# Moving VectorE work of the first batches of a linear-attention and mixer kernel to GpSimd and ScalarE

## The chip, the cores and the metric

One Trainium2 chip, one core. The time is device microseconds of one execution of the whole program; less is better. The engines are TensorE (PE in the profile), VectorE (DVE), ScalarE (ACT), GpSimd (POOL) and SyncE (SP, here only a queue of DMA issues).

## The reference

Three stages on 8 batches of 576 tokens and 512 channels (8 heads of 64), all float32:

```
q_s = softmax(q, over head_dim);  k_s = softmax(k, over tokens)
kv  = einsum('bhsd,bhse->bhde', k_s, v);  x = einsum('bhsd,bhde->bhse', q_s, kv)
xk  = mu_k*x + (1-mu_k)*x_prev;  xr = mu_r*x + (1-mu_r)*x_prev     # x_prev: one token earlier
x1  = sigmoid(xr @ w_r) * (maximum(xk @ w_k, 0)**2 @ w_v)
u   = x1 + real(fft(fft(x1, axis=1), axis=2))
out = u + maximum(layernorm(u) @ w_ch1, 0) @ w_ch2
```

The weights of the second and third stage come as float64.

## The kernel before, in words

Every large product is done as three matmuls on float32r parts: a value is rounded to its high part, the low part is value less high part, and high x high, low x high and high x low are summed in PSUM. A float64 weight is loaded as raw integers, turned into float32 by two ScalarE (L69, L73) and two VectorE instructions (L74, L77), and split by a ScalarE cast (L83) and a GpSimd subtraction (L84). Five raw buffers go round, so the next weight load, issued by SP, waits for an L84.

The first part of the program, on which the change acts, is attention and the first mixing, batch by batch:

- Keys, per batch and head pair (`hp` 0 to 3): `k_load`, `k_max` (VectorE maximum over the tokens within a partition), `k_col` (TensorE transpose, VectorE maximum `kc` for each channel, then `kd`, the identity with its rows scaled by `kc`), `k_sub` (a matmul of `ones` with `kd` spreads the maxima over all partitions; VectorE subtracts them from the keys), `k_exp` (ScalarE), `k_kv` (TensorE), `k_out` (VectorE reciprocal `rs`, then `kvh` on ScalarE and `kvl` on VectorE).
- Queries, per batch and group of tokens (`L`, `T`, `B`): `q_load`, `q_max` (VectorE), `q_sub` (subtracts the maximum), `q_exp` (ScalarE), `q_sum` (VectorE), `q_mul` (GpSimd), `q_tr` (TensorE transposes, high part on ScalarE, low part on VectorE), `q_x` (product with `kvh`, `kvl`; ScalarE copies it into `xb`, one buffer for each parity of batch).
- Mixing, per chunk `c` of 384 tokens (three chunks in two batches) and head pair: `mix_diff` forms the difference of a token and its neighbour (`dt`), `mix_part` forms `xm = dt*(1-mu) + x` once for `xk` and once for `xr` and splits each (`hi` on ScalarE, `lo` on GpSimd). Then `m_wk` (L440 to L442, eight column blocks), `m_r` (L456 to L458) and `m_wv` (L471 to L473).

Batch 0 and chunk 0 stand first in the program text, with the weight pieces behind them; batch 1 and all later work is placed by slots (`sched`, `aux`) between the matmuls of the chunk before. The text's order is not the last word: the program is built with

```
    with tile.TileContext(nc, schedule_with_timeline_sim=True) as tc:
```

so that the order of each engine's queue is planned at build from a model of the costs. Each queue then runs in order.

After this part come the two transforms (as matmuls with tables) and the last product, which fill the second half of the time with TensorE work.

The functions that the diff touches, with their line numbers:

Of the kernel before, what the change touches and what calls it, by code (L numbers as in the profile page):

```python
# [14 lines left out]
AF = mybir.ActivationFunctionType  # L15
ALU = mybir.AluOpType
# [26 lines left out]
def kernel(ctx, tc, q, k, v, mu_k, mu_r, w_k, w_v, w_r, w_ch1, w_ch2, tab_s, tab_d, out):  # L43
    nc = tc.nc
# [7 lines left out]
    ident = const.tile([P, P], F32, name="ident")  # L52
# [35 lines left out]
    with ExitStack() as ph:  # L88
# [20 lines left out]
        def spare(i, dtype, name):  # L109
            return wp.tile([P, 2 * D], dtype, tag=f"wv{i}", name=name, bufs=1)  # L110
# [5 lines left out]
        xb = [p1.tile([P, NHP, XW], F32, name=f"xb{i}") for i in range(2)]  # L116
# [5 lines left out]
        omu = p1.tile([P, 2, NHP], F32, name="omu")  # L122
# [64 lines left out]
        def k_col(n, hp):  # L187
            km = state.pop(("km", n, hp))
            pm = ps.tile([P, 512], F32, tag="pa", name=f"pm{n}_{hp}", bufs=4)
            nc.tensor.transpose(pm[:, 0:P], km, ident)  # L190
            kc = p1.tile([P, 1], F32, tag="kc", name=f"kc{n}_{hp}", bufs=2)
            nc.vector.tensor_reduce(out=kc, in_=pm[:, 0:P], axis=AX.X, op=ALU.max)
            kd = p1.tile([P, P], F32, tag="kd", name=f"kd{n}_{hp}", bufs=2)
            nc.vector.tensor_scalar(kd, ident, kc, None, op0=ALU.mult)
            state["kd", n, hp] = (kd, pm)

        def k_sub(n, hp):
# [71 lines left out]
        def q_sub(n, g):  # L269
            qt = state["q", n, g]  # L270
            np_, nj = qt.shape[0], qt.shape[2]
            qm = state.pop(("qm", n, g))
            (nc.vector if n < 2 else nc.gpsimd).tensor_tensor(
                out=qt,
                in0=qt,
                in1=qm[:np_, :, :nj].unsqueeze(3).to_broadcast([np_, H, nj, DH]),
                op=ALU.subtract,
            )
# [87 lines left out]
        done = set()  # L366

        KST = [k_load, None, k_max, k_col, k_shift, k_kv, k_out]
        QST = [q_load, None, None, q_max, q_sub, q_exp, q_sum, q_mul, q_tr, q_x]


# [24 lines left out]
        def mix_diff(c, hp):  # L396
            p, i = divmod(c, 3)
            for n in NEED[i]:
                for g in "LTB":
                    assert (2 * p + n + 2, g) not in done, (c, n, g)  # L400
            if c == 0:
                dt = spare(hp, F32, f"dt{c}_{hp}")[:, 0:CW]
            else:
                dt = p1.tile([P, CW], F32, tag="dt", name=f"dt{c}_{hp}", bufs=2)
            for o, w, par, xc, xp in REG[i]:
                x = xb[par]
                (nc.vector if c == 0 else nc.gpsimd).tensor_tensor(
                    out=dt[:, o : o + w], in0=x[:, hp, xp : xp + w], in1=x[:, hp, xc : xc + w], op=ALU.subtract
                )
            state["dt", c, hp] = dt  # L410

        def mix_part(c, hp, which):
            i = c % 3
            dt = state["dt", c, hp]
            hi, lo = ((xk_hi, xk_lo), (xr_hi, xr_lo))[which]
            xm = p1.tile([P, CW], F32, tag="xm", name=f"xm{c}_{which}_{hp}", bufs=2)
            for o, w, par, xc in MERGED[i]:
                nc.vector.scalar_tensor_tensor(  # L418
                    out=xm[:, o : o + w],
                    in0=dt[:, o : o + w],  # L420
                    scalar=omu[:, which, hp : hp + 1],
                    in1=xb[par][:, hp, xc : xc + w],
                    op0=ALU.mult,
                    op1=ALU.add,
                )
            nc.scalar.copy(hi[:, hp], xm)  # L426
            nc.gpsimd.tensor_tensor(out=lo[:, hp], in0=xm, in1=hi.bitcast(F32)[:, hp], op=ALU.subtract)  # L427

        def mix(c, hp):
            mix_diff(c, hp)  # L430
            for which in range(2):
                mix_part(c, hp, which)
# [80 lines left out]
        for n in range(1, B):  # L513
            p, par = divmod(n, 2)
# [18 lines left out]
        with tc.tile_pool(name="wst", bufs=1) as wst:  # L533
            for hp in range(NHP):
                for i, fn in enumerate((k_load, k_max, k_col, k_shift, k_kv, k_out)):
                    fn(0, hp)
                    if i == 0 and hp == 0:
                        for g in "TBL":
                            q_load(0, g)
                if hp < 3:  # L540
                    for fn in (q_max, q_sub, q_exp, q_sum, q_mul, q_tr):
                        fn(0, "TBL"[hp])
            for g in "LTB":
                q_x(0, g)
            xr_hi = p1.tile([P, NHP * CW], F32R, tag="xr0", name="xr_hi", bufs=1).rearrange("p (c n) -> p c n", c=NHP)
            mix_check(0)
            for hp in range(NHP):
                mix_diff(0, hp)
                mix_part(0, hp, 0)
            for hp in range(NHP):  # L550
                mix_part(0, hp, 1)
            for i, pc in enumerate(pieces):
                raw, ld = w_raw(wst, nc.sync, pc)
                if i < NRAW:
                    after(ld, early[0])
                if i == NF1 + NK:
                    for j in range(NF1):
                        t = spare(j, F32R, f"wv{j}").rearrange("p (f n) -> p f n", f=2)
                        (wv_hi if j < NF1 // 2 else wv_lo).append(t)
                ins = w_split(raw, pc)  # L560
                if i == 5:
                    early[1] = ins.ins.name
# [437 lines left out]
```

## Time and profile before

| | |
|---|---|
| median of 3 runs | 1659.78 us (1656.45 to 1660.05) |
| profiled execution | 1658.34 us |
| its span, first to last instruction | 1656.6 us |
| TensorE busy | 1537.8 us (93%) |
| VectorE busy | 728.3 us (44%) |
| ScalarE busy | 595.3 us (36%) |
| GpSimd busy | 511.7 us (31%) |
| mean granted TensorE clock | 0.98 of full speed |

The shares are averages over the whole span. A time in the rows below counts from the start of the span; "idle before <-releaser" is the time in which the engine stood just before that instruction, and what ended it. An instruction's duration runs from its start to its end, so an instruction that stands for another engine in the middle shows a longer one.

### The profile page before, as it was taken

What the parts mean: (1) busy time and instruction counts of PE and PEld (TensorE: products, weight loads), DVE (VectorE), ACT (ScalarE), POOL (GpSimd) and SP (SyncE); (2) the same over time, 40 slices, a digit from 0 to 9 for tenths busy, and PEclk for the clock granted to TensorE, in tenths of its full rate; (3) what the DMA queues carried; (4) which work ended last, traced back from release to release, by engine and by line L of the source; (5) the groups of instructions that cost most, each with busy time, mean ns of one, the idle gap of its engine ahead of it and who ended that gap; (6) DMA issues with size and microseconds to landing.
All of it is one profiled execution on the core that took longest, in us unless ns stands there. A gap on an engine that the chain in (4) does not pass through costs nothing.

```text
span 1656.6 us, 19891 instructions
## 1 busy us (share of the span) xinstructions
PE 1537.8 (93%) x7560; PEld 1309.2 (79%) x7560; DVE 728.3 (44%) x1302; ACT 595.3 (36%) x1120; POOL 511.7 (31%) x564
## 2 busy tenths in 40 slices
PE   2488999899989999968888999999999999999998
PEld 2476899788878899868866888888888888888886
DVE  8965544645364633089798312222231323131211
ACT  4673766466656564323554111111111111111110
POOL 4363663646265545275154101001010101010000
PEclk9698999999999999989999999999999999999999
DMA  7521312222221200465453201002020202010000
GB/s 200 163 84 50 81 56 66 72 57 65 53 77 55 67 13 11 152 224 168 162 186 127 77 1 58 19 14 64 1 77 1 77 1 77 0 51 0 26 1 26
DMA packets 120807, 114.27 MB, mean 69 GB/s; under 512 B 55144, under 2 KB 92136, under 8 KB 120456
## 3 DMA queue, kind: packets, MB, share of 16 engines
q1 hardware_dynamic: 113560, 94.97, 19.4%
q10 hardware_dynamic: 5184, 9.44, 1.6%
q0 software_dynamic: 1968, 8.60, 1.4%
q8 instruction: 59, 0.97, 0.2%
q14 instruction: 36, 0.29, 0.1%
HBM read 88.82 MB, written 24.16 MB: 68 GB/s over the span
## 4 chain that ended last, share of the span: by engine, by line
PE 42%; issue 7%; DVE 1%; POOL 1%; DMA 1%; ACT 0%; POOLq 0%; DVEq 0%; ACTq 0%; SPq 0%
PE ph L856 7%; PE ph L857 7%; PE ph L858 7%; PE pc L905 7%; PE pc L904 7%; PE pc L903 7%; DMA raw<-in_moe_w_ch_dram 1%; PE pt L845 1%; POOL w1l L84 1%; POOL w2l L84 1%; PE pd L758 1%; PE pz L724 1%; DVE raw L74 0%; DVE raw L71 0%; ACT raw L69 0%
## 5 line engine op out<-in xcount | busy, mean ns | idle before, releaser
L862 DVE SCALAR_TENSOR_TENSOR hl<-ph,hh 128x512 fp32r<-128x512 f32 x144 | 99.2, 689 | 431.7 <-ACT hh L861 431.7
L861 ACT ACTIVATE hh<-ph 128x512 fp32r<-128x512 f32 x144 | 86.1, 598 | 516.0 <-PE ph L858 516.0
L905 PE MATMUL pc<-w2h,hl 128*128 128x512 f32 x576 | 223.5, 392 | 9.0 <-DVE hl L862 9.0
L903 PE MATMUL pc<-w2h,hh 128*128 128x512 f32 x576 | 225.2, 391 | 3.8 <-ACT hh L861 3.8
L904 PE MATMUL pc<-w2l,hh 128*128 128x512 f32 x576 | 224.7, 390 | 0.0
L887 POOL DMA_INDIRECT out_dram<-ua,rev x16 | 15.9, 991 | 667.3 <-DVE hl L862 311.4
L418 DVE SCALAR_TENSOR_TENSOR xm<-dt,omu,xb 128x63 f32<-128x63 f32 (+4 forms) x224 | 117.3, 573 | 85.3 <-POOL xr_lo L427 35.1
L448 POOL TENSOR_TENSOR kk_lo<-h,kk_hi 128x384 fp32r<-128x384 f32 x96 | 98.8, 1033 | 147.7 <-ACT h L447 126.4
L440 PE MATMUL pk<-xk_hi,wk_hi 128*128 128x384 f32 x384 | 130.0, 347 | 11.7 <-ACT xk_hi L426 10.7
L905 PEld LDWEIGHTS pc<-w2h,hl 128*128 128x128 f32 x576 | 107.7, 188 | 35.1 <-DVE hl L862 12.5
L441 PE MATMUL pk<-xk_lo,wk_hi 128*128 128x384 f32 x384 | 131.6, 343 | 0.2 <-POOL xk_lo L427 0.2
L903 PEld LDWEIGHTS pc<-w2h,hh 128*128 128x128 f32 x576 | 108.1, 188 | 29.8 <-ACT hh L861 6.4
L442 PE MATMUL pk<-xk_hi,wk_lo 128*128 128x384 f32 x384 | 130.3, 340 | 0.0
L856 PE MATMUL ph<-uha,w1h 128*128 128x512 f32 x320 | 127.0, 399 | 0.0
L858 PE MATMUL ph<-uha,w1l 128*128 128x512 f32 x320 | 126.9, 397 | 0.0
L857 PE MATMUL ph<-ula,w1h 128*128 128x512 f32 x320 | 126.6, 396 | 0.0
L904 PEld LDWEIGHTS pc<-w2l,hh 128*128 128x128 f32 x576 | 108.1, 188 | 23.1
L471 PE MATMUL pv<-wv,kk_hi 128*128 128x512 f32 x288 | 113.1, 394 | 0.7 <-ACT sgt L460 0.7
L472 PE MATMUL pv<-wv,kk_hi 128*128 128x512 f32 x288 | 113.0, 394 | 0.0
L473 PE MATMUL pv<-wv,kk_lo 128*128 128x512 f32 x288 | 112.4, 393 | 0.0
L856 PE MATMUL ph<-uhb,w1h 128*128 128x512 f32 x256 | 100.6, 395 | 0.0
L858 PE MATMUL ph<-uhb,w1l 128*128 128x512 f32 x256 | 99.7, 390 | 0.0
(204 smaller groups left out, 3171.9 us busy)
## 6 DMA issues: line engine op xcount, KB each, us to landing
raw<-in_moe_w_ch_dram SPq DMA_DIRECT2D x32, 512.0 KB
x1d<-sgt ACTq DMA_DIRECT2D x36, 256.0 KB
ua<-x1d SPq DMA_DIRECT2D x36, 256.0 KB
wl<-wad SPq DMA_DIRECT2D x32, 258.0 KB
kt<-in_k_dram SPq DMA_DIRECT2D x32, 256.0 KB
xtt<-x1d SPq DMA_DIRECT2D x8, 1024.0 KB
vt<-in_v_dram SPq DMA_DIRECT2D x60, 128.0 KB
wad<-wa SPq DMA_DIRECT2D x16, 258.0 KB
```

Source lines behind the costliest of these rows:

```text
L418: nc.vector.scalar_tensor_tensor(out=xm[:, o : o + w], in0=dt[:, o : o + w], scalar=omu[:, which, hp : hp + 1], in1=xb[par][:, hp, xc : xc ...
L440: nc.tensor.matmul(pk, wh, xk_hi[:, kt], start=kt == 0, stop=False)
L441: nc.tensor.matmul(pk, wh, xk_lo[:, kt], start=False, stop=False)
L442: mm = nc.tensor.matmul(pk, wl, xk_hi[:, kt], start=False, stop=kt == NK - 1)
L471: nc.tensor.matmul(pv, kk_hi[f][:, ts], wv_hi[f // 2][:, f % 2], start=f == 0, stop=False)
L472: nc.tensor.matmul(pv, kk_hi[f][:, ts], wv_lo[f // 2][:, f % 2], start=False, stop=False)
L856: nc.tensor.matmul(ph_, w1h[f][:, kt], uh[:, kt], start=kt == 0, stop=False)
L857: nc.tensor.matmul(ph_, w1h[f][:, kt], ul[:, kt], start=False, stop=False)
L858: nc.tensor.matmul(ph_, w1l[f][:, kt], uh[:, kt], start=False, stop=kt == NK - 1)
L903: nc.tensor.matmul(a, hh[:, cs], w2h[f], start=f == 0, stop=False)
L904: nc.tensor.matmul(a, hh[:, cs], w2l[f], start=False, stop=False)
L905: nc.tensor.matmul(a, hl[:, cs], w2h[f], start=False, stop=f == NF2 - 1)
```

## The change

Four pieces of elementwise work change their engine. The scaling of the identity (`kd`) moves from VectorE to ScalarE, in all batches. The subtraction in `q_sub` moves from VectorE to GpSimd for batches 0 and 1 (for the others it was there). The differences of chunk 0 in `mix_diff` move from VectorE to GpSimd (for the other chunks they were there). The second mixing of chunk 0 (`which == 1`, for `xr`) was one VectorE instruction for each head pair; it becomes a scaling on ScalarE and an addition on GpSimd.

```
@@ k_col
-            nc.vector.tensor_scalar(kd, ident, kc, None, op0=ALU.mult)
+            nc.scalar.activation(out=kd, in_=ident, func=AF.Copy, scale=kc)
@@ q_sub
-            (nc.vector if n < 2 else nc.gpsimd).tensor_tensor(
+            nc.gpsimd.tensor_tensor(
@@ mix_diff
-                (nc.vector if c == 0 else nc.gpsimd).tensor_tensor(
+                nc.gpsimd.tensor_tensor(
@@ mix_part
+            if c == 0 and which == 1:
+                nc.scalar.activation(out=xm, in_=dt, func=AF.Copy, scale=omu[:, which, hp : hp + 1])
             for o, w, par, xc in MERGED[i]:
+                if c == 0 and which == 1:
+                    nc.gpsimd.tensor_tensor(
+                        out=xm[:, o : o + w], in0=xm[:, o : o + w], in1=xb[par][:, hp, xc : xc + w], op=ALU.add
+                    )
+                    continue
                 nc.vector.scalar_tensor_tensor(
```

## Rows read from the trace of the kernel before

**Rows 1.** The page, part 1: busy time, share of the span, instructions.

```profile
PE 1537.8 (93%) x7560; PEld 1309.2 (79%) x7560; DVE 728.3 (44%) x1302; ACT 595.3 (36%) x1120; POOL 511.7 (31%) x564
```

**Rows 2.** Busy time by stretch: length, engines, granted clock, DMA share, GB/s.

```profile
60.00:80.00 20.00, 10.26 (x43) 8.99 (x42) 19.52 (x35) 11.05 (x25) 6.99 (x10) 0.50 0.21 72
...
130.00:180.00 50.00, 41.82 (x208) 36.28 (x207) 32.54 (x74) 24.32 (x50) 26.11 (x36) 0.86 0.25 65
180.00:310.00 130.00, 127.88 (x700) 114.38 (x699) 64.00 (x117) 78.44 (x147) 67.89 (x76) 0.99 0.24 66
```

**Rows 3.** Waits of TensorE, 0 to 180 us: total, times, longest (us).

```profile
PE pm L200 <- DVE kd L194: 10.7, 5, 3.0
...
PE pk L440 <- ACT xk_hi L426: 6.1, 1, 6.1
...
PE ptB L332 <- POOL qeB L305: 5.1, 1, 5.1
```

**Rows 4.** Timeline of VectorE: start, duration (us), instruction.

```profile
23.66 0.68 DVE L296 TENSOR_REDUCE qsL<-qeL 64x8 f32<-64x512 f32 x1 [0.62 <-POOL qeT L305]
...
31.77 1.83 DVE L77 SCALAR_TENSOR_TENSOR raw<-raw 128x512 int32<-128x512 int32 x1
...
40.45 0.28 DVE L192 TENSOR_REDUCE kc<-pm 128x1 f32<-128x128 f32 x1
...
42.74 0.27 DVE L194 TENSOR_SCALAR kd<-ident,kc 128x128 f32<-128x128 f32 x1
...
68.95 0.15 DVE L231 RECIPROCAL rs<-rs 128x1 f32<-128x1 f32 x1
...
78.27 1.14 DVE L418 SCALAR_TENSOR_TENSOR xm<-dt,omu,xb 128x384 f32<-128x384 f32 x2
```

**Rows 5.** Timeline of GpSimd.

```profile
21.73 1.90 POOL L305 TENSOR_TENSOR qeT<-qeT,qsT 128x1024 f32<-128x1024 f32 x1 [15.09 <-DVE qsB L297]
23.59 1.90 POOL L305 TENSOR_TENSOR qeB<-qeB,qsB 128x1024 f32<-128x1024 f32 x1
...
31.75 1.30 POOL L84 TENSOR_TENSOR wk_lo<-raw,wk_hi 128x512 fp32r<-128x512 f32 x1 [4.83 <-ACT wk_hi L83]
...
73.05 2.68 POOL L407 TENSOR_TENSOR dt<-xb 128x63 f32<-128x63 f32 x5 [6.89 <-ACT xb L357]
75.68 1.03 POOL L305 TENSOR_TENSOR qeL<-qeL,qsL 64x512 f32<-64x512 f32 x1
...
84.55 1.01 POOL L427 TENSOR_TENSOR xk_lo<-xm,xk_hi 128x384 fp32r<-128x384 f32 x1 [1.04 <-ACT xk_hi L426]
...
97.20 1.06 POOL L427 TENSOR_TENSOR xr_lo<-xm,xr_hi 128x384 fp32r<-128x384 f32 x1
```

**Rows 6.** Timeline of ScalarE.

```profile
40.56 0.62 ACT L340 CAST qhB<-ptB 128x512 fp32r<-128x512 f32 x1
...
69.79 0.59 ACT L361 COPY xb<-pxB 128x512 f32<-128x512 f32 x1
...
73.49 0.64 ACT L361 COPY xb<-pxB 128x512 f32<-128x512 f32 x1
78.91 1.04 ACT L426 CAST xk_hi<-xm 128x384 fp32r<-128x384 f32 x2 [4.78 <-DVE xm L418]
```

**Rows 7.** Busy time of `q_sub` (L273) alone: VectorE, GpSimd, clock, DMA, GB/s.

```profile
0.00:30.00 30.00, 3.10 (x3) 0.00 (x0) 1.00 0.82 204
...
165.00:185.00 20.00, 0.00 (x0) 4.84 (x3) 0.91 0.36 90
```

**Rows 8.** One line of the kernel, L77: minimum, median, maximum in ns.

```profile
L77 DVE SCALAR_TENSOR_TENSOR raw<-raw x52: 666/690/1827, 29.1 to 901.2; 128x512 int32<-128x512 int32 x52
```

**Rows 9.** `mix_diff` (L407) alone, VectorE and GpSimd; then all of GpSimd.

```profile
70.00:80.00 10.00, 3.65 (x8) 3.04 (x6) 0.50 0.00 0
158.00:172.00 14.00, 0.00 (x0) 2.97 (x6) 0.88 0.47 116
...
77.00:100.00 23.00, 17.70 (x16) 0.86 0.37 111
```

## The prediction

> **What bounds the kernel now.** I read the page's head first, then the busy times by stretch, then who TensorE waited for, then VectorE's, GpSimd's and ScalarE's own order of work around the last of these waits. TensorE is the bound, busy for 93% of the span [rows 1]. The change touches the attention and the first mixing, and there the question is where TensorE still idles. Between 180 and 310 us it works 127.88 of 130, so an engine that gets freer there gives nothing. Between 130 and 180 it loses 8.2 us. From 60 to 80 us it is busy half of the time, while VectorE is busy 19.52 of the 20 us [rows 2]. So the start is VectorE's: whatever brings the first matmul of chunk 0 (L440) forward moves all later TensorE work with it. That matmul waited 6.1 us for `xk_hi`; before it TensorE waited 10.7 us in sum for `kd` [rows 3].
>
> Batch 0 has a chain that runs once for each of four head pairs: transpose, `kc`, `kd`, ones matmul, `k_sub`, exp, `k_kv`, `k_out`. Its steps on VectorE stand in one queue with the queries of batches 0 and 1, the token differences and the splitting of the weights. Then come the last copy into `xb` (73.49 + 0.64 = 74.1 us), the differences, `xm`, `xk_hi` and, last, `xk_lo` of pair 3 at 84.55 + 1.01 = 85.56 us [rows 5, 6]. From the last `xb` to there it is 11.4 us.
>
> **The change part by part.** A gain is time by which TensorE's work from 80 us on moves forward.
>
> *Batch 0's query subtraction.* Three VectorE instructions, 3.10 us, become three on GpSimd, 4.84 us by the same shapes of batch 2 [rows 7]. GpSimd sat idle for 15.09 us ahead of 21.73, so it has room [rows 5]. Each subtraction gets longer, 1.7 us in all, but VectorE reaches the next group's `q_max` and pair 1's `k_max` sooner. The trace does not show when pair 1's keys landed, so the gain lies between 0 and 3.1. I take 2.5: VectorE hardly pauses from there on, and what is taken out shortens its queue. GpSimd's work is no brake here: VectorE's reduce at 23.66 us took 0.68 us beside a GpSimd multiplication that ran from 23.59 [rows 4, 5], and reduces are most of what VectorE has left there.
>
> *The identity's scaling.* 32 instructions leave VectorE, and ScalarE gets as many. In pair 2 `kc` ended at 40.73 us and `kd` ran from 42.74 to 43.01, behind other VectorE work. ScalarE was free at 41.18 (its cast began at 40.56, 0.62 long) [rows 4, 6]. The trace has no ScalarE copy of 128x128 from SBUF; half of that 128x512 cast, 0.3 us as an estimate from it, ends `kd` at 41.5: a gain of 1.5. The same three times (pairs 1 to 3) is the upper bound, 4.5. Below: ScalarE's queue is in order too, and one such cast more ahead of each `kd`, less the 0.27 us saved, makes -1.1. What then waits behind a `kd` that waits for `kc` are casts, exps and, later, ScalarE's stores. I take 1.5, one pair's worth, since `k_sub` still queues on VectorE. In batches 1 to 7 the 28 others have TensorE's nearly full work of 180 to 310 us as cover: 0, and about 1 us either way where that cover has a gap.
>
> *Batch 1's query subtraction.* It frees the same 3.1 us, just ahead of pair 3's reciprocal, which only started at 68.95 us and holds the last `kvh` [rows 4]. But here VectorE splits weights, and that collides: L77 took 1.83 us at 31.77, where GpSimd ran L84 from 31.75 for 1.30, against a usual 0.69 [rows 4, 5, 8]. Such a meeting cost 1.14 us for 1.30 us of GpSimd, 88%. At 4.84 us of GpSimd that is 4.3 lost for 3.1 freed: -1.2. If none meets, +3.1. I take -1.2, since weights are split throughout.
>
> *Chunk 0's token differences.* Eight VectorE instructions, 3.65 us, go to GpSimd, which later took 2.97 us for three pairs of the same sizes [rows 9]: 1.0 a head pair, 4.0 in all. The first two pairs can run before the last `xb`. After it GpSimd has two pairs of differences (2.0) and four `xk_lo` (4.0), and four `xm` may hold it up for 0.57 each (2.3; two took 1.14 undisturbed [rows 4]): 8.3 us in place of 11.4, a gain of 3.1. If all the `xm` fall into gaps it is 5.4. If the ready pieces of chunk 1 and batch 1's product (2.68 and 1.03 us, which now run from 73.05 us while GpSimd has nothing else [rows 5]) come in between, it is -0.6. I take 3.1.
>
> *Chunk 0's second mixing.* Four `xm` leave VectorE. Each becomes a scaling on ScalarE (0.5, by two `xk_hi` casts of 128x384 in 1.04 [rows 6]) and an addition on GpSimd (1.0, by `xk_lo`). What hides it is chunk 0's `pk` work, which TensorE does ahead of most of `m_r`. Before, the last `xr_lo` came at 98.26 us, and GpSimd did 17.70 us of work in the 23 from 77 to 100 [rows 5, 9]. Now it has 4.0 of differences, 4.0 of additions, 3.7 of ready pieces and 17.7, 29.4 us, from about 67.6 (the first half of group B was in `xb` at 69.79 + 0.59 [rows 6], less 2.8 by the three parts above): to 97.0. TensorE would want the last `xr_lo` 5.9 us sooner than 98.26 by the parts so far, at 92.4. If the weight splits in that stretch are put after it, nothing is late; if not, up to 4.6 us is lost. I take -1.0. No DMA is added. SP's weight loads wait for L84 to free their raw buffers, so a later L84 delays loads of `w_v`, which chunk 0 reads only in its last stage (`m_wv`): 0.
>
> Sum: 2.5 + 1.5 - 1.2 + 3.1 - 1.0 = 4.9 us. The profiled execution took 1658.34 us, so 1653.4; the median shown is 1.4 above it, so 1654.8 on its scale. All lower ends together (0 - 1.1 - 1.2 - 0.6 - 4.6, and 1 for the later batches) are 8.5 slower, all upper ends (3.1 + 4.5 + 3.1 + 5.4 + 0 + 1) 17.1 faster.
>
> **A rule against it.** The row at 31.77 us shows VectorE standing until GpSimd was nearly done with its instruction [rows 4, 5]. The Trainium skill, "SBUF — State Buffer", section "SBUF: two separate sides", says that VectorE instructions with two SBUF inputs and GpSimd instructions share one port pair as an exclusive lock, held for the whole instruction. The trace agrees here, and by that rule much of this move buys VectorE nothing; the second rival works out from rows what this gives.
>
> **The rivals.**
> *Slower: GpSimd becomes chunk 0's gate.* Its queue is in order. If the planner puts the differences (4.0), additions (4.0), three `xr_lo` (3.0), the ready pieces (3.7) and three weight splits (1.30 each, 3.9) ahead of the last of the four `xk_lo` (4.0), that is 22.6 us, with 2.3 of VectorE's `xm` 24.9, from 67.6: 92.5 against 85.56, so 6.9 us slower, 1666.7. It decides from 18 us of GpSimd work up to that `xk_lo`; 8 must be there. For it: each moved operation is longer on GpSimd. Against it: GpSimd idles 6.89 us before 73.05 [rows 5].
> *Same: what VectorE gives up it loses in waiting.* With 88% of each GpSimd operation lost: batch 1's queries -1.2, differences 3.65 - 0.88 x 4.0 = +0.1, additions 2.3 - 3.5 = -1.2, batch 0's queries and `kd` as above +4.0: 1.7 faster, 1658.1. For it: the row at 31.77. Against it: VectorE's reduces and what it reads from PSUM have no part in it, if they go on as the reduce at 23.66 did.
> *Slower, by order.* Every queue's order is planned anew at build. TensorE stood 5.1 us for batch 1's product [rows 3]; if the start gains nothing and such a wait comes once more, it is 1664.9.
>
> **How the numbers follow.** A measurement of this kernel tells about 0.2%, 3.3 us, from no change; the three runs shown span 3.6. The forecast and what lies beyond it hold 0.53, VectorE's waiting 0.27, GpSimd as the gate 0.13, the order 0.07. So faster 0.53, same 0.27, slower 0.20. The forecast's own range is 1646 to 1656.4. To leave out no more than 2 in 10 the range must take in the second rival and about half of the slower cases: 1646 to 1665.
>
> **What would show it.** Right: L440 starts at 73 to 76 us instead of after 79; `kd` follows `kc` within a microsecond; pair 3's reciprocal comes before 68; the differences lie on GpSimd ahead of `xk_lo` without idle time; TensorE's idle time before 180 us falls by 4 to 6, and the rest of the profile moves up unchanged. Wrong: L441 or L458 waiting on GpSimd at 80 to 100 us; L74 and L77 at 1.8 us and more in the stretch 55 to 75; `kd` behind stalled casts on ScalarE; or TensorE idling more around 140 us than before, which would eat the gain.

## The result, and the profile after

| | before | after |
|---|---|---|
| median | 1659.28 us (4 runs, 1656.45 to 1660.05) | 1644.19 us (4 runs, 1642.0 to 1644.8) |
| ratio, 95% interval | | 0.9912 (0.99 to 0.9925) |
| span of the profiled execution | 1656.6 us | 1642.0 us |

The change is 15.1 us faster; 4.9 were forecast, and the time lies below the range. The page's part 1 of the changed kernel, against [rows 1]:

```profile
PE 1534.3 (93%) x7560; PEld 1306.5 (80%) x7560; DVE 710.1 (43%) x1252; ACT 604.8 (37%) x1154; POOL 532.3 (32%) x582
```

Busy time by stretch, against [rows 2]. From 60 to 80 us TensorE is hardly better off; from 130 to 180 it now works 48.70 of 50 in place of 41.82, at a granted clock of 1.00 in place of 0.86:

```profile
130.00:180.00 50.00, 48.70 (x264) 43.00 (x263) 32.40 (x68) 31.83 (x63) 34.19 (x46) 1.00 0.26 71
60.00:80.00 20.00, 11.27 (x43) 9.20 (x42) 18.34 (x27) 11.31 (x25) 16.69 (x19) 0.50 0.32 106
```

TensorE's waits in the first 130 us, against [rows 3]. The wait for `kd` did not shrink, and there is a new one for GpSimd's `xr_lo`:

```profile
PE pm L200 <- ACT kd L194: 20.6, 7, 5.8
...
PE pr L466 <- POOL xr_lo L435: 1.4, 1, 1.4
```

The 20.6 us are not to be set against the 10.7 of [rows 3] alone. In the kernel before one wait of the same line, for pair 2's `kd`, is put down to a DMA:

```profile
PE pm L200 <- DMA raw<-in_moe_w_k_dram: 5.1, 1, 5.1
```

The matmul that it ends started at 43.07 us, just behind the `kd` that ended at 43.01 [rows 4]. With it the wait went from 15.9 to 20.6 us: from 12.2 to 14.8 in batch 0, and from 3.7 to 5.8 in batch 1.

GpSimd's timeline, against [rows 5]. Batch 1's three subtractions (groups `L`, `T`, `B`) with a weight split between them, then twelve differences in one block (of chunk 0's eight and six ready pieces of chunk 1); the last `xk_lo` and the last `xr_lo` of chunk 0:

```profile
60.91 1.44 POOL L273 TENSOR_TENSOR ql<-ql,qmL 64x512 f32<-64x512 f32 x1 [1.37 <-DMA qtB<-in_q_dram]
62.31 1.28 POOL L84 TENSOR_TENSOR wr_lo<-raw,wr_hi 128x512 fp32r<-128x512 f32 x1
65.36 2.29 POOL L273 TENSOR_TENSOR qtT<-qtT,qmT 128x1024 f32<-128x1024 f32 x1 [1.76 <-DVE qmT L266]
68.29 2.36 POOL L273 TENSOR_TENSOR qtB<-qtB,qmB 128x1024 f32<-128x1024 f32 x1 [0.64 <-DVE qmB L266]
70.62 7.89 POOL L407 TENSOR_TENSOR dt<-xb 128x128 f32<-128x128 f32 x12
...
85.38 1.01 POOL L435 TENSOR_TENSOR xk_lo<-xm,xk_hi 128x384 fp32r<-128x384 f32 x1 [1.04 <-ACT xk_hi L434]
...
107.69 1.05 POOL L435 TENSOR_TENSOR xr_lo<-xm,xr_hi 128x384 fp32r<-128x384 f32 x1
```

The last `xb` comes 4.6 us earlier (ScalarE's timeline below: 68.95 + 0.61 = 69.56, before 74.13 [rows 6]). But the last `xk_lo` ends at 86.39 us, 0.8 later than before, and the last `xr_lo` at 108.74, 10.5 later [rows 5].

```profile
50.98 0.42 ACT L194 ACTIVATE kd<-ident,kc 128x128 f32<-128x128 f32 x1
...
68.95 0.61 ACT L361 COPY xb<-pxB 128x512 f32<-128x512 f32 x1
...
75.49 0.49 ACT L434 CAST xk_hi<-xm 128x384 fp32r<-128x384 f32 x1
```

Nor does TensorE's first matmul of chunk 0 (L440 of the kernel before, L448 here) wait for the mixing any more. Its first `xk_hi` was there at 75.49 + 0.49 = 75.98 us, but batch 1's first head pair stands ahead of it in TensorE's queue, with two waits of its own:

```profile
72.01 0.80 PE L200 MATMUL pm<-kd,ones 128*128 128x128 f32 x2 [3.29 <-ACT kd L194]
75.64 2.54 PE L223 MATMUL pkv<-vt,ek 128*128 128x130 f32 x10 [2.83 <-ACT ek L209]
...
78.04 0.99 PE L448 MATMUL pk<-xk_hi,wk_hi 128*128 128x384 f32 x2
```

So chunk 0 did not gain. The gain shows in TensorE's timeline where batch 1 is finished. First the kernel before: the last of chunk 0's `m_wv`, then the transposes of batch 1's groups T and B, then chunk 1's first matmul:

```profile
136.12 0.39 PE L473 MATMUL pv<-wv,kk_lo 128*128 128x512 f32 x1
136.65 1.09 PE L332 MATMUL ptT<-ident,qeT 128*128 128x128 f32 x8
...
144.09 1.97 PE L332 MATMUL ptB<-ident,qeB 128*128 128x128 f32 x8 [5.09 <-POOL qeB L305]
...
150.68 0.61 PE L440 MATMUL pk<-xk_hi,wk_hi 128*128 128x384 f32 x2
```

Then the changed kernel:

```profile
119.25 1.04 PE L332 MATMUL ptT<-ident,qeT 128*128 128x128 f32 x8
...
130.78 1.04 PE L332 MATMUL ptB<-ident,qeB 128*128 128x128 f32 x8
...
139.85 0.39 PE L481 MATMUL pv<-wv,kk_lo 128*128 128x512 f32 x1
140.09 0.27 PE L190 MATMUL pm<-ident,km 128*128 128x128 f32 x1
140.11 0.60 PE L448 MATMUL pk<-xk_hi,wk_hi 128*128 128x384 f32 x2
```

Before, both transposes come after chunk 0's last matmul, so the softmax of each group (exp, sum, product on three engines) runs while TensorE has little or nothing to do. After, they stand between chunk 0's matmuls, and chunk 1 follows chunk 0 at once: 10.6 us earlier, though chunk 0 ends 3.7 us later. TensorE's clock shows it too: 256-wide products of `q_x` follow each other by 0.21 us before (145.71 to 148.21) and by 0.12 after (131.57 to 132.95).

A further 3.5 us come between the first matmul of chunk 1 and that of chunk 3. TensorE is busy for 102.38 us with 543 matmuls there before, at a granted clock of 0.97, and for 99.04 us with 541 after, at 1.00. Before, then after:

```profile
150.68:254.57 103.89, 102.38 (x543) 91.07 (x542) 61.98 (x120) 63.58 (x120) 67.91 (x79) 0.97 0.25 66
...
140.11:240.45 100.34, 99.04 (x541) 88.72 (x540) 56.43 (x105) 66.55 (x126) 64.28 (x71) 1.00 0.26 71
```

Where the 14.6 us of TensorE's last matmul lie, from both traces: up to the first matmul of chunk 3 -14.1 (254.6 to 240.5 us); from there to the end of chunk 11 +1.6; to the transforms' first matmul +0.7; in the transforms -3.9 (104.1 to 100.3); behind them +1.1. The 14.1 do not all last: at chunk 4's first matmul 10.9 are left (308.5 to 297.7), for between the two the changed kernel has the lower clock, 0.97 against 1.00, and a wait of 2.1 us for a later batch's queries against one of 0.5. At the end of chunk 11 it is 12.5.

### The profile page after: what moved, and what is told of

Its sections match the earlier page's. It is cut to its first block, busy times and chain, and to the rows that moved or that the text cites. A ratio compares the mean times of both kernels' runs of the same rounds, so it can differ in the third digit from the quotient of the medians.

```text
span 1642.0 us, 19900 instructions
## 1 busy us (share of the span) xinstructions
PE 1534.3 (93%) x7560; PEld 1306.5 (80%) x7560; DVE 710.1 (43%) x1252; ACT 604.8 (37%) x1154; POOL 532.3 (32%) x582
## 4 chain that ended last, share of the span: by engine, by line
PE 72%; issue 9%; DVE 9%; DMA 3%; POOL 3%; ACT 2%; SPq 1%; POOLq 0%; ACTq 0%; DVEq 0%
PE ph L866 7%; PE ph L864 7%; PE ph L865 7%; PE pc L913 7%; PE pc L912 7%; PE pc L911 7%; PE pk L450 3%; PE pk L449 3%; PE pk L448 3%; PE pv L479 3%; PE pv L481 3%; PE pv L480 3%; DVE xm L426 2%; PE pz L732 2%; PE pr L464 2%
## 5 line engine op out<-in xcount | busy, mean ns | idle before, releaser
L870 DVE SCALAR_TENSOR_TENSOR hl<-ph,hh 128x512 fp32r<-128x512 f32 x144 | 99.3, 690 | 432.0 <-ACT hh L869 432.0
L895 POOL DMA_INDIRECT out_dram<-ua,rev x16 | 15.9, 993 | 667.2 <-DVE hl L870 311.5
L448 PE MATMUL pk<-xk_hi,wk_hi 128*128 128x384 f32 x384 | 128.9, 345 | 8.2 <-ACT xk_hi L434 5.1
```

Of the source, the lines that this page charges most:

```text
L448: nc.tensor.matmul(pk, wh, xk_hi[:, kt], start=kt == 0, stop=False)
```

## The experiments

Two theories at first. *A:* the gain is that batch 1's keys and queries ("batch 1's chain") are worked off while TensorE still has chunk 0's 204 matmuls. *B:* each part relieves VectorE by itself, as the prediction summed it. The places given in the expectations are those in TensorE's queue as built.

**One part alone.**

```
kd_only:    k_col      nc.vector.tensor_scalar(kd, ...) -> nc.scalar.activation(kd, ...)
qsub_only:  q_sub      (nc.vector if n < 2 else nc.gpsimd) -> nc.gpsimd
dt_only:    mix_diff   (nc.vector if c == 0 else nc.gpsimd) -> nc.gpsimd
xm_only:    mix_part   c == 0 and which == 1: ScalarE scaling + GpSimd addition
```

> Before with the identity's scaling alone on ScalarE. Theory A (batch 1's chain: the gain is that batch 1's keys and queries are worked off while TensorE still has chunk 0's 204 matmuls, so that chunk 1 no longer waits): the built queue has the first transposes of batch 1's group T behind all 204 matmuls of chunk 0, as before, so no gain, within 2 us of before. Theory B (VectorE's relief before 75 us, each part by itself, as the prediction summed it): about 1.5 us faster.

> Before with the queries' subtraction of batches 0 and 1 alone on GpSimd. Theory A: group T of batch 1 still stands behind all 204 matmuls of chunk 0, so no gain, within 2 us of before. Theory B: 2.5 - 1.2 = 1.3 us faster.

> Before with chunk 0's token differences alone on GpSimd. Theory A: group T of batch 1 comes after 180 of the 204 matmuls, 24 earlier, at 0.23 us each 5.5 us faster. Theory B: 3.1 us faster, by an earlier first matmul of chunk 0.

> Before with chunk 0's second mixing alone on ScalarE and GpSimd. Theory A: group T of batch 1 comes after 180 of the 204 matmuls, so about 5.5 us faster. Theory B: 1 us slower.

**One part taken back** from the changed kernel (the same four lines, each reversed).

> The changed kernel with the identity's scaling back on VectorE. Theory A: batch 1's chain stands in TensorE's queue just where the changed kernel has it (group T after 134 of chunk 0's 204 matmuls, group B after 175), so nearly the whole gain stays, 13 to 15 us faster than before. Theory B: the scaling's 1.5 us are lost, and 13 left; a third theory C, that the scaling is what shortens each pair's chain (TensorE waited 10.7 us for it in before), would lose 5 us or more.

> The changed kernel with the queries' subtraction of batches 0 and 1 back on VectorE. Theory A: group T after 145, group B after 186 of the 204 matmuls, 11 later than in the changed kernel but still ahead of chunk 0's end: 10 to 15 us faster than before. Theory B: loses 1.3 of the gain.

> The changed kernel with chunk 0's differences back on VectorE. Theory A: group T after 198, group B behind all 204 matmuls, nearly as before: 1 to 4 us faster than before, most of the gain lost. Theory B: loses 3.1, so 11 to 12 us faster than before.

> The changed kernel with chunk 0's second mixing back on VectorE. Theory A: group T after 176, group B behind all 204: 5 to 8 us faster than before, half of the gain lost. Theory B: gains 1 more than the changed kernel, 15 to 16 us faster than before.

What was measured. The first column is the ratio to before; then, from each trace, when group B's transposes of batch 1 start, when chunk 0's last matmul ends, when chunk 1, chunk 3 and chunk 4 start, and what TensorE still needs from chunk 3's start to its last matmul (us). All kernels have done the same 1239 matmuls when chunk 4 starts; when chunk 3 starts it is 950 or 952, but 915 in `slow_noxm` further down. The stretches are those of one execution of each kernel, and the times of one kernel's executions lie 1.1 (`after_h2`) to 5.8 us (`hold0`, `q0_after`) apart, so a few us in one stretch of one kernel prove little:

```
            ratio (95%)              B of batch 1  chunk 0 ends  chunk 1  chunk 3  chunk 4  rest
before      1                            144.1        136.5      150.7    254.6    308.5    1395.0
after       0.9912 (0.9900 - 0.9925)     130.8        140.2      140.1    240.5    297.7    1394.5
no_kd       0.9954 (0.9940 - 0.9969)     129.9        139.4      139.3    240.1    294.1    1403.1
no_qsub     0.9952 (0.9935 - 0.9968)     134.0        140.6      140.7    242.1    296.3    1401.8
kd_only     0.9968 (0.9958 - 0.9978)     142.0        133.5      148.7    250.8    304.7    1395.0
qsub_only   1.0050 (1.0033 - 1.0066)     143.4        135.4      150.1    253.6    307.5    1401.5
dt_only     1.0036 (1.0022 - 1.0050)     138.0        138.1      143.0    247.4    304.5    1406.4
xm_only     0.9979 (0.9970 - 0.9989)     139.8        137.6      144.7    248.9    308.3    1398.3
no_dt       1.0018 (1.0009 - 1.0028)     139.7        135.9      146.5    249.8    308.7    1405.2
no_xm       0.9957 (0.9940 - 0.9973)     136.1        135.8      141.1    245.7    302.8    1398.5
```

As sums of parts the times make no sense: the four single moves are 5.4 and 3.5 us faster and 6.8 and 5.1 slower, together slower, while all four together are 15 faster. As times the expectations were nearly all missed: of the eight theory A had `no_xm` right, theory B none. Read at chunk 3's start, a point chosen after the times were known, the runs do make sense and agree with theory A but for one: nearly the whole 14 us without the scaling or the queries, a third without the differences, two thirds without the second mixing, and from the single moves little (1 to 7). The exception is `kd_only`: its chain stands behind chunk 0 as before, yet chunk 3 starts 3.8 us earlier, with L440 2.9 and chunk 0's end 3.0 earlier. Theory B had 1.5, 1.3, 3.1 and -1.0 for the single moves, and for the runs with a part taken back nothing like 9 us lost with the differences. What theory A did not have is the rest, which scatters over 12 us and turned `dt_only` and `no_dt`, ahead at chunk 3, slower than before; at chunk 4 `no_dt` and `xm_only` have already lost what they were ahead.

One part of that scatter has a place. In five of these runs (`qsub_only`, `dt_only`, `no_kd`, `no_qsub`, `no_dt`) the queue has 52 of chunk 10's matmuls behind chunk 11's first, in the others 26. Waits of TensorE from 560 to 730 us, `dt_only`:

```profile
PE pz L724 <- ACT fht L698: 13.1, 1, 13.1
PE pk L440 <- ACT xk_hi L426: 2.7, 4, 1.3
```

and the changed kernel:

```profile
PE pz L732 <- ACT fht L706: 9.6, 1, 9.6
```

With 52 the transforms' first matmul waits 11.8 to 13.2 us, with 26 it waits 8.8 to 10.3 (all 20 kernels), and `dt_only` has 2.7 us of waits for mixed inputs besides, which the changed kernel has not. Most of the scatter lies ahead of that wait, though: from chunk 3's start to the end of chunk 11 the 20 kernels take 449.8 to 464.5 us, and what sets that is open.

**The chain held up, and the order at the end.**

```
hold0, hold3 (on the changed kernel):
-            nc.scalar.activation(out=kd, in_=ident, func=AF.Copy, scale=kc)
+            kdi = nc.scalar.activation(out=kd, in_=ident, func=AF.Copy, scale=kc)
+            if n == 1 and hp == 0:
+                after(kdi, held[0, 0, 0])        # hold3: held[0, 0, 3]; held: the lo subtractions of mix_part
q0_after:   q_sub   nc.gpsimd -> (nc.gpsimd if n != 1 else nc.vector)
nokd_late:  k_col   ScalarE for n < 2 alone
```

> The changed kernel, and batch 1's first scaling of the identity also waits for chunk 0's first low part of xk; nothing changes its engine. Theory A: group L of batch 1 then has 161 of chunk 0's 204 matmuls ahead of it (changed kernel 94, before 172) and group T all 204, so most of the gain at the start goes: 4 to 8 us faster than before. Theory B (VectorE's relief): one operation is held, VectorE has as little work as in the changed kernel, so within 3 us of the changed kernel, 12 us or more faster than before.

> As hold0, but it waits for chunk 0's last low part of xk. Theory A: group L has 190 matmuls ahead of it, later than before (172): the gain at the start is gone or turned round, between 4 us faster and 4 slower than before. Theory B: within 4 us of the changed kernel.

> The changed kernel with batch 1's query subtraction back on VectorE. Theory A: group L after 151, group T after 198 of the 204 matmuls, the end of the mixing in the order of before (26 of chunk 10's matmuls behind the first of chunk 11): 4 to 8 us faster than before. Theory B: 1.2 us faster than the changed kernel.

> The changed kernel with the scaling of batches 2 to 7 back on VectorE. The built queue has batch 1's chain exactly where the changed kernel has it, but at the end of the mixing the other of two orders that the planner uses (52 matmuls of chunk 10 behind the first of chunk 11 in place of 26). Theory A with that order as a second term: the start gain stays, 7 us are lost at the end, so 6 to 9 us faster than before. Without such a term: as the changed kernel, 14 to 15 us faster than before.

```
            ratio (95%)              B of batch 1  chunk 0 ends  chunk 1  chunk 3  chunk 4  rest
hold0       1.0013 (1.0003 - 1.0022)     146.7        139.5      153.4    256.4    315.6    1394.8
hold3       0.9961 (0.9947 - 0.9975)     144.6        134.6      151.1    253.5    307.4    1393.4
q0_after    0.9959 (0.9946 - 0.9971)     141.1        137.3      147.6    249.9    304.0    1390.4
nokd_late   0.9955 (0.9938 - 0.9971)     129.5        139.0      138.8    240.2    294.1    1399.5
```

Holding one 0.4 us operation turns the start's gain into a loss of 1.8 us (`hold0`) or leaves 1.1 of it (`hold3`), with every moved operation on its new engine. Theory B falls here, by either run. Theory A missed both as times: `hold0` is 2 us slower than before, not 4 to 8 faster, and `hold3` 6 faster, not within 4. Its expectation for `q0_after` held: 7 us faster, 4.7 at chunk 3. Waits of TensorE in `hold0` from 60 to 160 us show the wait of before for batch 1's group B, unchanged in length [rows 3]:

```profile
PE pk L451 <- ACT xk_hi L437: 6.9, 1, 6.9
PE ptB L334 <- POOL qeB L307: 5.1, 1, 5.1
```

`nokd_late` has the changed kernel's start and loses 5.0 us in the rest, 7 in the median, as theory A with the order at the end expected. 3.3 of the 5.0 are the transforms' wait, which goes with that order; 0.6 lie from chunk 3 to the end of chunk 11, where the 24 scalings stand that it takes back.

**Why does the chain come forward?** *A1:* VectorE is freed, so batch 1's steps run sooner. *A2:* chunk 0's mixed inputs come later on the slower engines, so the planner puts batch 1's chain ahead of chunk 0's matmuls. Two runs give VectorE its work back, two go further the same way.

```
slow_noxm (on no_xm), behind xm in mix_part:
+            if c == 0 and which == 1:
+                nc.scalar.activation(out=xm, in_=xm, func=AF.Copy, scale=1.0)
+                x3 = xm.rearrange("p (a b) -> p a b", b=P)
+                nc.gpsimd.tensor_tensor(out=x3, in0=x3, in1=ones.unsqueeze(1).to_broadcast([P, 3, P]), op=ALU.mult)
dum_dve (on the changed kernel), ahead of ScalarE's scaling:
+                dum = p1.tile([P, CW], F32, tag="dum", name=f"dum{hp}", bufs=1)
+                nc.vector.scalar_tensor_tensor(out=dum, in0=dt, scalar=omu[:, 1, hp : hp + 1], in1=xb[0][:, hp, X_T : X_T + CW], ...)
after_h1:   if c == 0 and which == 1  ->  if c == 0 and (which == 1 or hp > 2)        # after_h2: hp > 1
```

> The run no_xm (second mixing of chunk 0 whole on VectorE; 7.7 us faster than before) and, behind each of its four instructions, a ScalarE copy and a GpSimd multiplication by ones that change nothing: VectorE has its work back and two engines have useless work more. Theory A1 (VectorE is freed): as no_xm or slower, 4 to 8 us faster than before. Theory A2 (chunk 0's mixed inputs come later, so batch 1's chain is put ahead of its matmuls): the queue has group T after 129 and group B after 172 of the 204 matmuls (changed kernel 134 and 175), so 13 to 16 us faster than before, in spite of the extra work.

> The changed kernel with four additional VectorE instructions of the size of those that the second mixing gave up, whose results nobody reads. Theory A1: VectorE is no freer than in no_xm, so 5 us or more of the gain are lost. Theory A2: batch 1's chain keeps its place (group L after 94, T after 134, B after 175), so within 2 us of the changed kernel, 13 to 15 us faster than before.

> The changed kernel with the first mixing of chunk 0's last head pair also moved to ScalarE and GpSimd. Theory A2: group L of batch 1 stands after 66 matmuls in place of 94, group T after 126 in place of 134, B after 168 in place of 175; chunk 1 waits no more in the changed kernel, so nothing is left to gain there and TensorE waits longer for chunk 0: from 2 us faster to 4 slower than the changed kernel. Theory A1: 0.6 us faster than the changed kernel.

> The same for the last two head pairs: group L after 94, group T after 141, group B after 178. Theory A2: as the changed kernel, within 3 us of it. Theory A1: 1.1 us faster than the changed kernel.

```
            ratio (95%)              B of batch 1  chunk 0 ends  chunk 1  chunk 3  chunk 4  rest
slow_noxm   0.9968 (0.9956 - 0.9980)     137.8        150.1      142.8    242.4    307.1    1403.9
dum_dve     0.9930 (0.9916 - 0.9944)     131.9        141.3      141.2    241.5    299.5    1399.7
after_h1    0.9947 (0.9933 - 0.9961)     132.4        144.6      144.4    243.2    307.5    1400.3
after_h2    0.9912 (0.9899 - 0.9926)     131.0        140.5      140.3    242.7    299.6    1394.9
```

VectorE's timeline in `dum_dve` shows the work that it got back, a little ahead of where `no_xm` has the second mixing (83.95 to 93.73 us):

```profile
74.82 0.61 DVE L420 SCALAR_TENSOR_TENSOR dum<-dt,omu,xb 128x384 f32<-128x384 f32 x1
...
76.72 0.61 DVE L420 SCALAR_TENSOR_TENSOR dum<-dt,omu,xb 128x384 f32<-128x384 f32 x1
...
80.20 2.02 DVE L420 SCALAR_TENSOR_TENSOR dum<-dt,omu,xb 128x384 f32<-128x384 f32 x2
```

Chunk 3 still starts 13 us earlier than before: with the work back on VectorE, 4.2 of the 5.3 us between `no_xm` and the changed kernel stay, at chunk 4 3.4 of 5.2. So the relief of VectorE is not the main worth of the second mixing's move at the start; against A1, `dum_dve` is 11.4 us faster than before, which is less than A2 expected and more than A1 did.

`slow_noxm` was to show A2 and does not. Its chunk 3 starts 12.1 us earlier than before, but 24 matmuls of the chunks before then stand behind chunk 3's first one in TensorE's queue, in no other kernel any: the order moved, and not the work. Those chunks end at 249.5 us, in `no_xm` at 245.9 and before at 254.7, and chunk 4 starts 1.4 us earlier than before, in `no_xm` 5.7. The time, 4.6 us faster, is what A1 expected (4 to 8), not A2 (13 to 16). Here the delay came with useless work on two engines, so it does not refute A2 either. What the second mixing's move does at the start is thus open between its delay and something else; by `dum_dve` VectorE's relief is the smaller part.

`after_h1` missed its expectation: it is about 6 us slower than the changed kernel, not between 2 faster and 4 slower, and loses nearly all of its start between chunk 3 and chunk 4, 8.7 us of it in one wait for a later batch's queries. `after_h2` equals the changed kernel. Nothing tried beats it.

**A control, and the pair.**

```
kd_late:  k_col   ScalarE for n >= 2 alone (on before)
dt_xm:    the lines of dt_only and xm_only together (on before)
```

> Before with the identity's scaling of batches 2 to 7 alone on ScalarE. Batch 1's chain stands where before has it. Theory A2 with scatter by order: chunk 3 starts within 2 us of before, and the rest may move the time by up to 5 us either way. If the rest were steady: within 1 us of before.

> Before with chunk 0's differences and second mixing moved, and nothing else. The queue has group L after 121, group T after 174 of chunk 0's 204 matmuls, group B behind them (single moves 180, changed kernel 134 and 175), and the other order at the end (52). Theory A2: chunk 3 starts 6 to 10 us earlier than before, more than with one of the two alone (7.2 and 5.7) and less than in the changed kernel (14.1); with 5 to 8 lost at the end the time is 5 faster to 2 slower than before. If the two alone made the whole gain: chunk 3 starts 13 to 15 us earlier.

```
            ratio (95%)              B of batch 1  chunk 0 ends  chunk 1  chunk 3  chunk 4  rest
kd_late     0.9972 (0.9960 - 0.9984)     143.9        136.4      150.6    252.8    306.7    1390.1
dt_xm       1.0064 (1.0050 - 1.0078)     141.7        141.3      146.6    251.0    308.5    1408.8
```

The control changes next to nothing at the start (1.8 us) and is 5 us faster. Of the 4.9 us in its rest only 1.5 lie from chunk 3 to the end of chunk 11, where the moved scalings stand, and 2.4 in the transforms, where none does. An order planned anew is the likely cause, but no run changes the order and nothing else. `dt_xm` missed its expectation (chunk 3 3.6 us earlier in place of 6 to 10; in time 11 us slower than before, slower than any other run). The pair alone delays chunk 0 (141.3) but does not bring group B ahead of its end. With either of the other two parts it does: `no_kd` 129.9, `no_qsub` 134.0.

Over all 20 kernels one line divides the start, with one exception. In seven of them (the changed kernel, `no_kd`, `no_qsub`, `nokd_late`, `dum_dve`, `after_h1`, `after_h2`) group B's transposes start more than 6 us ahead of chunk 0's end, and chunk 3 starts 11.4 to 14.5 us earlier than before; at chunk 4 six of them keep 8.9 to 14.5, `after_h1` 1.0. In eleven others that changed something they start from level with it to 10 us behind it, and chunk 3 starts between 8.9 earlier and 1.8 later. The exception is `slow_noxm`, where they are 12 us ahead of chunk 0's end because that end is put off.

## Why the prediction was wrong

The step that failed is the first paragraph's "whatever brings the first matmul of chunk 0 (L440) forward moves all later TensorE work with it", with "the rest of the profile moves up unchanged" behind it. L440 came at 78.04 us, 1.4 earlier, and chunk 0 ended 3.7 later than before. The gain lies between chunk 0 and chunk 1, in the 8.2 us that TensorE lost from 130 to 180 us and the 5.1 us wait for batch 1's product [rows 2, 3]. The prediction quoted both, booked no gain there, and used the wait for a rival on the slow side. Other runs show the same: in `q0_after` L440 starts 7.2 us earlier than before, the earliest of all, and chunk 3 4.7 earlier; in `hold0` L440 starts 4.5 earlier and chunk 3 1.8 later. In a few runs the two do go together (`kd_only` 2.9 and 3.8, `qsub_only` 1.8 and 1.0).

That the change was faster at all, as forecast, owes little to the forecast's sum: 1.4 of the 4.9 us came about where the sum has them. By this part the direction is luck.

One reading was wrong as well. Of the 10.7 us of waits for `kd` "before it", 3.7 belong to batch 1 and come behind L440 (at 90.83 and 106.76 us), and the 5.1 us that the profile puts down to a DMA are left out.

Term by term:

- *Batch 0's queries (+2.5), `kd` (+1.5), batch 1's queries (-1.2):* together 2.8 at the last `xb`; measured 4.6. The other runs separate them. The queries of both batches bring the last `xb` 4.7 us forward (`qsub_only` 69.42 us against 74.13 before; the changed kernel against `no_qsub`, 74.28, the same). Batch 1's alone cost 1.5 (`q0_after` 68.08), close to the forecast, so batch 0's are worth about 6 by difference, more than the upper end of 3.1. `kd` gives 0.3 alone (`kd_only` 73.85) and costs 0.7 in the changed kernel (`no_kd` 68.91). The scaling took 0.40 us, not 0.3, and from the end of `kc` to the end of `kd` pair 1 went from 1.35 to 0.4 us, pairs 2 and 3 stayed at 2.2 and 2.0: ScalarE's queue took VectorE's place. Batch 1's collisions cost VectorE 3.7 us, priced at 4.3. L77 at 61.47 us met group L's subtraction and the weight split behind it, L74 at 68.81 group B's subtraction; group T's held up no VectorE instruction. Its timeline:

```profile
61.47 2.68 DVE L77 SCALAR_TENSOR_TENSOR raw<-raw 128x512 int32<-128x512 int32 x1
...
65.20 0.68 DVE L74 SCALAR_TENSOR_TENSOR raw<-raw 128x512 int32<-128x512 int32 x1
...
68.13 0.68 DVE L77 SCALAR_TENSOR_TENSOR raw<-raw 128x512 int32<-128x512 int32 x1
...
68.81 2.39 DVE L74 SCALAR_TENSOR_TENSOR raw<-raw 128x512 int32<-128x512 int32 x1
```

- *Differences (+3.1):* wrong in sign for chunk 0. From the last `xb` to the last `xk_lo` it took 16.8 us, not 8.3 (before 11.4). The differences are 2 us of that: 13.2 with them alone (`dt_only`), 14.7 with all but them (`no_dt`). What the lower bound named happened: chunk 1's ready pieces ran inside the block of twelve, and batch 1's subtractions stood just ahead of it. The rest is the sum's own error: an earlier last `xb` does not bring the last `xk_lo` forward. In `qsub_only`, with the differences on VectorE, the first came 4.7 us earlier and the second at the time of before (85.53 us).
- *Second mixing (-1.0):* chunk 0's last `xr_lo` was 10.5 us late; TensorE waited 1.4 us for it, since batch 1's work stood between chunk 0's matmuls by then. Chunk 3's start loses 5.3 us when this part is taken back (240.5 to 245.7), and 9.4 when the differences are. So the part booked as a small loss, and the one booked as a gain at the wrong place, carry most of the start, and neither does so by an earlier chunk 0.
- *Later scalings (0, within 1):* the control moved by 5 us. The bound was for the work moved, and most of the 5 us lie where none of it stands.
- *The rivals.* GpSimd did hold up chunk 0's low parts (its queue ran without a gap from 68.29 us to the first two `xk_lo` at 80.18), and it did not make the kernel slower, since TensorE had batch 1's work to do meanwhile. VectorE's waiting was there too, 3.7 us of it. A change that leaves the start alone can move the time by as much as the whole forecast (`kd_late`); a newly planned order was named with 0.07 and on the slow side alone, which was too little and one-sided.

So of the 15 us the start holds 14.1 up to chunk 3, of which 10.9 are left at chunk 4, shown by the runs that move it. -0.4 net is what the rest adds, with 3.9 gained in the transforms, where before was the longest of all 20 kernels (104.1 against 99.3 to 102.2 us). These 3.9 are not the change's doing by any mechanism shown: every other kernel gains 1.9 to 4.8 there, the control too.

That the gain is batch 1's chain slipping under chunk 0 is shown by `hold0` and `hold3`, which hold back one scaling of that chain and move no work. What brings the chain forward is open for the differences, which carry the most and were never tested apart from VectorE's relief, and for the second mixing as said above. Also open is what sets the rest, 1390 to 1409 us, beyond the order at the end.

## What to carry to other kernels

Before costing a move from a bound engine, find each place in the first stage where the matrix engine idles, and ask what the next batch is waiting for there; a move that makes the current batch later can pay if the next batch's chain slips under it. Where a planner sets the queues' order, parts do not add up: look first at who stands ahead of whom in the matrix engine's queue, and take a control that moves work far from the place in question before a few tenths of a per cent are put down to a cause. Compare such runs by stretches, not by the time alone, and end a stretch where every kernel has the same work behind it: chunk 3's start misled about `slow_noxm`, chunk 4's did not.

## What the runs showed of the hardware

Collisions between GpSimd and VectorE cost the one that came second, on either side. Batch 1's two large subtractions (1.90 us for 128x1024 in batch 2; all three there 4.84 [rows 7]) took 2.29 and 2.36 us on GpSimd where a VectorE weight split (L74 at 65.20, L77 at 68.13, both 0.68) was already running. L77 and L74 took 2.68 and 2.39 us on VectorE, in place of 0.69 for L77 [rows 8], where GpSimd's operations were running; L74 ended at 71.20, 0.55 behind the subtraction that it met. It isn't only instructions with two inputs: in the kernel before a 64x8 VectorE operation with one (0.16 us for the same at 70.22) stood beside GpSimd's multiplication of 23.59 to 25.49 us [rows 5], right behind the reduce that did not:

```profile
24.37 1.14 DVE L297 TENSOR_SCALAR qsL<-qsL 64x8 f32<-64x8 f32 x1
```

So the prediction's "GpSimd's work is no brake here" holds for the reduces alone.

TensorE's granted clock fell while it stood: in the kernel before its mean is 0.74 over the 5.09 us wait (139.00 to 144.09 us), and right behind it 0.50, the lower of its two levels (1.2 of 2.4 GHz):

```profile
144.09:146.00 1.91, 1.91 (x9) 1.91 (x10) 0.00 (x0) 0.00 (x0) 0.00 (x0) 0.50 0.00 0
```

The changed kernel has 1.00 from 100 to 200 us, and its products ran at the 0.12 us steps given above in place of 0.21.
